# Agent attention and a gated feed-forward layer on one core: the SBUF tiles laid out in another order

## The chip, the cores and the metric

The kernel runs on 1 core of one Trainium2 chip. The metric is the device time of one execution in microseconds (us). The kernel before takes 1909.14 us, the median of 3 runs (1908.99 to 1910.31).

## What is computed

The reference, cut to what matters. Four batches of 12480 tokens, 128 channels, 49 agents; the 49920 result tokens go through a layer of width 2048.

```python
def sm(a, b):
    s = scale * (a @ b.transpose(0, 2, 1))
    s = s - s.max(-1, keepdims=True)
    e = np.exp(s)
    return e / (e.sum(-1, keepdims=True) + 1e-09)
agent_v = sm(agents, k) @ v
q2a = sm(q, agents)
x = (q2a @ agent_v).reshape(49920, 128)
h = x @ w_in
g = h * (1.0 / (1.0 + np.exp(-1.702 * h)))
return g @ w_out
```

## The kernel before

The kernel never forms the attention result x. For each batch it folds `agent_v` into the first weight matrix (`weights_part`, lines 492 to 507), so that a token's 49 softmax weights are multiplied with a 49 x 2048 matrix. Every float32 factor of the two large products is split in two parts (a rounded high part and the rest) and three products are added: high by high, low by high, high by low.

- **Up** (`up`, lines 580 to 593): for a chunk of 512 tokens and two slices of 128 of the 2048 columns, six matmuls into two PSUM banks `ph`. The weights `wh` and `wl` are the stationary operands, `hi`, `lo` (or their copies `hi2`, `lo2` with the halves of the partitions exchanged) the moving ones. Slice k stands on partitions k*64 to k*64+48, so the two matmuls of a pair work on the two halves of TensorE's rows.
- ScalarE applies the activation into `g` (line 591). `gh`, the rounded copy of `g`, comes from a DMA that POOL issues (line 601) or from ScalarE (line 603). VectorE makes `gl = g - gh` (line 609).
- **Down** (`down`, lines 612 to 619): twelve matmuls for two slices, weights `wo_h`, `wo_h`, `wo_l` against `gh`, `gl`, `gh`, again in pairs on the two halves of the rows, added up in `po`.
- Between these, in places that a table written out by hand sets, stand the softmax scores in bf16 pieces (line 241: `ag_part` against `qt`, `kt` and their remainders `rest`), the sum over the values (line 117 with `v_pair` and `e_pair`), a running maximum and the transposes of `p_pad`.

All these matmuls go through `on_rows` (line 117) or line 241. The engines' orders come from the order of the calls alone; no scheduler moves anything.

Every tile belongs to a pool. The pools lie in SBUF one behind another in the order in which they are opened, and inside a pool the tiles lie in the order in which they are first asked for, each rounded up to 32 bytes. So a tile whose size is no multiple of 256 bytes shifts everything that comes behind it modulo 256. Five such tiles stand in the pool `const`, more of them in the pool `work`:

```python
ag_sb = const.tile([P, B, A], F32, name="ag_sb")                    # 784 bytes a partition
v_pair = const.tile([P, KB, 2 * C + 2], F32R, name="v_pair")        # 8256
e_sb = const.tile([P, KB, A + 1], F32, name="e_sb")                 # 1600
score = const.tile([P, NKG * KB, A], F32, name="score")             # 20384
max_b = const.tile([P, A], F32, name="max_b")                       # 196
```

One tile walks through the bytes by itself: `v_pair` holds eight rows of 258 numbers, 1032 bytes each, and starts at byte 160 modulo 256. The eight matmuls of a group read them one after another, so their moving operands start at bytes 160, 168, 176, 184, 192, 200, 208 and 216 modulo 256. `score` does the same for VectorE: its slices for the 13 groups of keys begin 1568 bytes apart, so 32 further on modulo 256 each.

Of the kernel before, what the change touches and what calls it, by code (L numbers as in the profile page):

```python
# [8 lines left out]
F32 = mybir.dt.float32  # L9
F32R = mybir.dt.float32r  # L10
BF16 = mybir.dt.bfloat16
I32 = mybir.dt.int32
U32 = mybir.dt.uint32
# [5 lines left out]
P = 128  # L19
TB = 120  # L20
KB = 8
KG = TB * KB
QB = 128
CH = 512
# [25 lines left out]
def kernel(  # L50
# [11 lines left out]
    B, C, N = qT.shape  # L62
    A = agT.shape[2]
# [5 lines left out]
    NKG = N // KG  # L69
    H = P // 2  # L70
# [5 lines left out]
    def width(m):  # L76
        return min(CH, T - m * CH)
# [11 lines left out]
    const = ctx.enter_context(tc.tile_pool(name="const", bufs=1))  # L89
    wpool = ctx.enter_context(tc.tile_pool(name="wpool", bufs=2))  # L90
    loads = ctx.enter_context(tc.tile_pool(name="loads", bufs=3))
    work = ctx.enter_context(tc.tile_pool(name="work", bufs=2))
    gpool = ctx.enter_context(tc.tile_pool(name="gpool", bufs=3))
    ps_h = ctx.enter_context(tc.tile_pool(name="ps_h", bufs=4, space=bass.MemoryType.PSUM))
    ps_o = ctx.enter_context(tc.tile_pool(name="ps_o", bufs=1, space=bass.MemoryType.PSUM))
    ps_m = ctx.enter_context(tc.tile_pool(name="ps_m", bufs=1, space=bass.MemoryType.PSUM))
# [8 lines left out]
    def one_bank():  # L105
        return ps_h.tile([P, 512], F32, name="ph")

    def bank_pair(ps):
        ps = two_banks() if ps is None else ps
        return [ps[:, 0], ps[:, 1]]  # L110

    def rows(k, n=H):
        return slice(k * H, k * H + n)
# [2 lines left out]
        r = rows(k, n)  # L116
        nc.tensor.matmul(out=out, lhsT=lhsT[r], rhs=rhs[r], start=start, stop=stop, tile_position=(k * H, 0))  # L117

    ag_sb = const.tile([P, B, A], F32, name="ag_sb")
    nc.sync.dma_start(out=ag_sb, in_=agT)  # L120

    ident = const.tile([P, P], F32, name="ident")
# [5 lines left out]
    for i in range(2):  # L128
        t = const.tile([P, KB, P], F32R, name=f"e_pair{i}")
        nc.gpsimd.memset(t.bitcast(F32), 0.0)  # L130
        e_pair.append(t)
    v_pair = const.tile([P, KB, 2 * C + 2], F32R, name="v_pair")
    nc.gpsimd.memset(v_pair[:, :, 2 * C :].bitcast(F32), 1.0)
    p_pad = const.tile([P, KB // 2, P], F32, name="p_pad")
    nc.gpsimd.memset(p_pad, 0.0)


    e_sb = const.tile([P, KB, A + 1], F32, name="e_sb")
    nc.gpsimd.memset(e_sb[:, :, A:], EPS)

    w_in_sb = const.tile([P, F], F32, name="w_in_sb")
    wo_h = const.tile([P, NF, C], F32R, name="wo_h")
    wo_l = const.tile([P, NF, C], F32R, name="wo_l")
    score = const.tile([P, NKG * KB, A], F32, name="score")
    max_b = const.tile([P, A], F32, name="max_b")

# [5 lines left out]
    def to_float32(w, out):  # L154
        lo = w.rearrange("p n w -> p (n w)").bitcast(U16).rearrange("p (n w) -> p n w", w=4)[:, :, 1]
        hi = w[:, :, 1]
        ts = nc.vector.tensor_scalar
        stt = nc.vector.scalar_tensor_tensor

        ex = work.tile([P, 512], I32, name="ex", tag="rest")  # L160
        ts(out=ex.bitcast(U32), in0=hi, scalar1=20, scalar2=0x7FF, op0=ALU.logical_shift_right, op1=ALU.bitwise_and)
        yield
        ts(out=ex, in0=ex, scalar1=1023 - 127, scalar2=1023 + 128, op0=ALU.max, op1=ALU.min)
        yield
        ts(out=ex, in0=ex, scalar1=float(127 - 1023), scalar2=float(1 << 23), op0=ALU.add, op1=ALU.mult)
        yield
        stt(out=ex.bitcast(U32), in0=hi, scalar=0x80000000, in1=ex.bitcast(U32), op0=ALU.bitwise_and, op1=ALU.bitwise_or)
        yield

        m = work.tile([P, 512], U32, name="m21", tag="o", bufs=1)  # L170
        ts(out=m, in0=hi, scalar1=0xFFFFF, scalar2=0x100000, op0=ALU.bitwise_and, op1=ALU.bitwise_or)
        yield
        stt(out=m.bitcast(F32), in0=m, scalar=float(1 << 16), in1=lo, op0=ALU.mult, op1=ALU.add)
        yield
        stt(out=out, in0=m.bitcast(F32), scalar=2.0**-36, in1=ex.bitcast(F32), op0=ALU.mult, op1=ALU.mult)
# [3 lines left out]
    def convert(k, n=7):  # L179
        if k not in conversions:  # L180
            out, i = WORDS[k]
            conversions[k] = to_float32(words.pop(k), (wo_f if out else w_in_sb)[:, i * 512 : (i + 1) * 512])
        for _ in range(n):
            next(conversions[k], None)
# [10 lines left out]
        wo, s = quarter(i)  # L195
        nc.vector.tensor_sub(out=wo_l[:, s, :], in0=wo, in1=wo_h[:, s, :].bitcast(F32))

    ag_part = const.tile([P, B, 3, A], BF16, name="ag_part")

    def split_agents():  # L200
        rest = ag_sb
# [7 lines left out]
    def halves(t):  # L209
        w = t.bitcast(BF16).rearrange("p (n w) -> p n w", w=2)  # L210
        return w[:, :, 1], w[:, :, 0]
# [3 lines left out]
    def split(t):  # L215
        n = t.shape[1]
        half = n // 2
        if n == KG + PAD:
            half = (n + PAD) // 2
            nc.gpsimd.memset(t[:, KG:], 0.0)  # L220
        r = work.tile([P, n], F32, name="rest", tag="rest")

        def piece(i):
            s = slice(0, half) if i < 2 else slice(half, n)
            if i % 2 == 0:
                nc.vector.tensor_sub(out=r[:, s], in0=t[:, s], in1=halves(t)[0][:, s])  # L226
            else:
                nc.vector.tensor_sub(out=halves(r)[1][:, s], in0=r[:, s], in1=halves(r)[0][:, s])  # L228

        return (halves(t)[0], halves(r)[0], halves(r)[1]), piece  # L230
# [110 lines left out]
    def factors_0():  # L341
        m = work.tile([P, 1], F32, name="mcol", bufs=1)
        nc.vector.tensor_reduce(out=m, in_=first_m, axis=AX.X, op=ALU.min)
        ps = one_bank()
        nc.tensor.transpose(out=ps[:1, :P], in_=m, identity=ident)
        r = work.tile([P, 2, P], F32, name="mrow", tag="hi")
        nc.vector.tensor_copy(out=r[:1, 0], in_=ps[:1, :P])
        a, b = (r[:1, 0, k * H : (k + 1) * H].unsqueeze(1).broadcast_to([1, 2, H]) for k in range(2))
        nc.vector.tensor_tensor(out=r[:1, 1].rearrange("p (c a) -> p c a", c=2), in0=a, in1=b, op=ALU.min)
        return r  # L350
# [31 lines left out]
        return rz  # L382

    def divided(ps, rz):
        avT = work.tile([P, P], F32, name="avT", bufs=1)
        nc.vector.tensor_tensor(
            out=avT.rearrange("p (c a) -> p c a", c=2),
            in0=ps.rearrange("p (c a) -> p c a", c=2),
            in1=rz.unsqueeze(1).broadcast_to([P, 2, H]),
            op=ALU.mult,  # L390
        )
        return avT
# [157 lines left out]
    def query_pairs(g, ps=None):  # L550
        pp = p_pad
        ps = bank_pair(ps)
        hi, lo, hi2, lo2 = (work.tile([P, CH], F32R, name=x) for x in ("hi", "lo", "hi2", "lo2"))
        parts = []
        for k, n in enumerate((H, QB - H)):
            for i in range(KB // 2):
                nc.tensor.transpose(  # L557
                    out=ps[k][:, i * n : (i + 1) * n],
                    in_=pp[rows(k, n), i, :],
                    identity=ident[rows(k, n), rows(k, n)],  # L560
                    tile_position=(k * H, 0),
                )
            t = [x.rearrange("p (i t) -> p i t", t=QB)[:, :, rows(k, n)] for x in (hi, lo)]
            parts.append((ps[k][:, : KB // 2 * n].rearrange("p (i t) -> p i t", t=n), *t))
        for x, h, _ in parts:
            nc.scalar.copy(out=h, in_=x)
        return parts, hi, lo, hi2, lo2
# [58 lines left out]

    def store(m, po):
        n = width(m)
        o = work.tile([P, 2, CH], F32, name="o", tag="o", bufs=1)[:, :, :n]
        out = outT[:, m * CH : m * CH + n]  # L630
        if m == NC - 1:
            nc.scalar.copy(out=o[:, 0], in_=po[:, 0, :n])
            nc.vector.tensor_add(out=o[:, 0], in0=po[:, 1, :n], in1=o[:, 0])
            nc.sync.dma_start(out=out, in_=o[:, 0])
            return None
        nc.scalar.copy(out=o, in_=po[:, :, :n])  # L636
        nc.sync.dma_start(out=out, in_=o[:, 0])
        return o
# [31 lines left out]
    def do_key_split(b, g, i):  # L670
        if i == 0:
            k_parts[b, g], pieces[b, g] = split(kts.pop((b, g)))
        pieces[b, g](i)

    def do_query_split(n, i):
        if n < NG:
            if i == 0:
                q_parts[n], pieces[n] = split(qts.pop(n))
            pieces[n](i)
# [61 lines left out]
    with tc.manual_schedule(engines={E.PE, E.Activation, E.DVE, E.Pool, E.SP}):  # L741
# [1 line left out]
        first_m, first_z = first_mz[:, 0:KP], first_mz[:, KP:].rearrange("p (k i) -> p k i", i=3)  # L743
        nc.vector.memset(first_z, 0.0)
        nc.scalar.activation(out=first_m[:, 0:1], in_=first_z[:, 0, 0:1], func=AF.Exp)
        ag_0 = work.tile([P, H], F32, name="ag_0", tag="avT", bufs=1)
        nc.vector.memset(ag_0, 0.0)
        nc.vector.memset(sel, 0.0)
        nc.vector.tensor_copy(out=ag_0[:, 0:A], in_=ag_sb[:, 0, :])
# [20 lines left out]
        for p in range(KP):  # L770
# [13 lines left out]
            for i, (g, e) in enumerate(zip(first_groups(p), cols_e)):  # L784
                first_sums(p, g, e)
                if p == KP - 2 and i == 0:
                    r = factors_0()
                if p == KP - 2 and i == 1:
                    f = factors_1(r)
                    zc = first_zc(f)  # L790
                    acc = work.tile([P, 2, 2 * C + 1], F32, name="acc", bufs=1)[:, 0, 0:C]
                if p == KP - 1 and i == 0:
                    rz = first_rz(zc)
# [243 lines left out]
```

## Time and profile before

| | us |
|---|---|
| median of 3 runs | 1909.14 |
| the profiled execution | 1908.36 |
| its span, first to last instruction | 1906.6 |
| TensorE (PE) busy | 1883.1 |
| weight loads (PEld) busy | 1759.4 |
| VectorE (DVE) busy | 1537.3 |
| ScalarE (ACT) busy | 1492.3 |

The profile is of one execution, 0.04% below the median of the runs. A matmul's record lasts from its start to its modelled end, which lies about 160 ns behind the point where the next one of the same half can start; so two records overlap, and how fast matmuls follow one another is read from their starts, or from the time and the count of a stretch. The mean granted clock of TensorE was 0.999.

### The profile page before, as it was taken

How to read it: one execution, taken by the hardware profiler on the slowest of the kernel's cores; microseconds unless marked ns; L12 is line 12 of the kernel's file. 1: busy time of each engine (PE TensorE's matmuls, PEld its weight loads, DVE VectorE, ACT ScalarE, POOL GpSimd, SP SyncE). 2: the span in 40 equal slices, each digit the busy share in tenths (PEclk: the TensorE clock that was granted, in tenths of full speed). 3: DMA queues.
4: the chain of work that ended last, by engine and by line, in shares of the span. 5: the costliest groups of instructions: out<-in, count | busy, mean ns of one | idle time of the engine just before them, and what ended most of it. 6: DMA issues, size and time to landing. Idle time of an engine off the chain costs nothing.

```text
span 1906.6 us, 56411 instructions
## 1 busy us (share of the span) xinstructions
PE 1883.1 (99%) x24100; PEld 1759.4 (92%) x24100; DVE 1537.3 (81%) x1978; ACT 1492.3 (78%) x2410; POOL 335.5 (18%) x591
## 2 busy tenths in 40 slices
PE   7999999999999999999999999999999999999999
PEld 4678889999899999999999998999989999999999
DVE  7888998888688889888778888898867677767765
ACT  3677777888787777878777778777878788888886
POOL 1111111111111111111111111111111111111111
PEclk9999999999999999999999999999999999999999
DMA  9576767776567677777657777767655666666665
GB/s 362 171 223 211 210 203 205 212 215 199 169 207 208 209 206 209 214 205 204 203 173 207 210 211 200 214 203 207 191 170 178 192 196 184 197 186 193 195 179 145
DMA packets 133500, 384.96 MB, mean 202 GB/s; under 512 B 15125, under 2 KB 16789, under 8 KB 133249
## 3 DMA queue, kind: packets, MB, share of 16 engines
q0 software_dynamic: 77776, 254.98, 47.0%
q1 hardware_dynamic: 55473, 126.38, 19.8%
q8 instruction: 189, 3.10, 0.7%
q14 instruction: 62, 0.51, 0.1%
HBM read 81.53 MB, written 50.99 MB: 70 GB/s over the span
## 4 chain that ended last, share of the span: by engine, by line
PE 88%; DVE 6%; DMA 3%; issue 2%; ACT 2%; POOL 0%; SPq 0%; POOLq 0%; DVEq 0%; ACTq 0%
PE po L117 53%; PE ph L117 26%; PE ps_m L241 5%; DVE gl L609 2%; PE ps_m L117 2%; DMA kt<-kT 1%; DVE rest L226 1%; ACT g L591 1%; DVE rest L228 1%; DMA gh<-g 1%; PE ps_m L503 1%; PE ps_m L557 1%; DMA words<-w_out 0%; DVE score L254 0%; DMA lo<-lo 0%
## 5 line engine op out<-in xcount | busy, mean ns | idle before, releaser
L591 ACT ACTIVATE g<-ph 128x512 f32<-128x512 f32 x1568 | 807.7, 604 | 296.9 <-PE ph L117 285.8
L609 DVE TENSOR_TENSOR gl<-g,gh 128x1024 fp32r<-128x1024 f32 x776 | 924.4, 1215 | 79.9 <-ACT gh L603 56.2
L117 PE MATMUL po<-gh,wo_h 64*128 64x512 f32 (+1 forms) x3104 | 547.7, 398 | 0.0
L117 PE MATMUL po<-gl,wo_h 64*128 64x512 f32 (+1 forms) x3104 | 537.9, 393 | 1.9 <-DVE gl L609 1.9
L117 PE MATMUL po<-gh,wo_l 64*128 64x512 f32 (+1 forms) x3104 | 534.0, 390 | 0.0
L601 POOL DMA_DIRECT2D gh<-g x436 | 239.8, 551 | 1401.0 <-ACT g L591 1117.9
L117 PEld LDWEIGHTS po<-gl,wo_h 64*128 64x128 f32 x3104 | 367.6, 184 | 18.5 <-DVE gl L609 8.1
L117 PEld LDWEIGHTS po<-gh,wo_l 64*128 64x128 f32 x3104 | 369.9, 185 | 12.2
L117 PE MATMUL ph<-hi,wh 49*128 49x512 f32 (+4 forms) x1616 | 368.1, 387 | 0.3 <-DVE wl L507 0.3
L117 PE MATMUL ph<-lo,wh 49*128 49x512 f32 (+4 forms) x1616 | 367.6, 388 | 0.1
L117 PE MATMUL ph<-hi,wl 49*128 49x512 f32 (+4 forms) x1616 | 365.5, 384 | 0.0
L603 ACT CAST gh<-g 128x1024 fp32r<-128x1024 f32 (+1 forms) x340 | 357.6, 1053 | 9.0
L117 PEld LDWEIGHTS po<-gh,wo_h 64*128 64x128 f32 x3104 | 350.0, 185 | 13.8 <-issue 5.6
L117 PEld LDWEIGHTS ph<-hi,wh 49*128 49x128 f32 x1616 | 203.9, 184 | 11.1 <-ACT g L591 2.5
L117 PEld LDWEIGHTS ph<-lo,wh 49*128 49x128 f32 x1616 | 203.4, 184 | 7.2 <-DMA lo<-lo 0.6
L117 PEld LDWEIGHTS ph<-hi,wl 49*128 49x128 f32 x1616 | 203.3, 186 | 7.3 <-issue 0.7
L636 ACT COPY o<-po 128x1024 f32<-128x1024 f32 x97 | 98.3, 1013 | 62.2 <-PE po L117 62.2
L228 DVE TENSOR_TENSOR rest<-rest 128x512 bf16<-128x512 f32 (+2 forms) x176 | 129.9, 745 | 0.9
L241 PE MATMUL ps_m<-ag_part,rest 64*128 64x49 bf16 x4188 | 120.4, 181 | 0.3 <-DVE rest L228 0.3
L241 PEld LDWEIGHTS <-rest 64*128 64x128 bf16 (+1 forms) x4236 | 113.0, 94 | 0.6 <-DVE rest L228 0.4
L254 DVE TENSOR_TENSOR e_sb<-ps_m,e_sb 128x392 f32<-128x392 f32 x48 | 27.1, 565 | 97.2 <-ACT e_sb L253 97.2
L642 POOL DMA_DIRECT2D outT<-o x97 | 86.2, 888 | 91.4 <-DMA outT<-o 58.8
(143 smaller groups left out, 1324.9 us busy)
## 6 DMA issues: line engine op xcount, KB each, us to landing
gh<-g POOLq DMA_DIRECT2D x434, 512.0 KB, 3.5
kt<-kT SPq DMA_DIRECT2D x52, 480.0 KB
outT<-o SPq DMA_DIRECT2D x97, 256.0 KB
outT<-o POOLq DMA_DIRECT2D x97, 256.0 KB, 4.1
qt<-qT SPq DMA_DIRECT2D x94, 256.0 KB
vt<-v SPq DMA_DIRECT2D x39, 480.0 KB
hi<-hi SPq DMA_DIRECT2D x96, 98.0 KB
lo<-lo SPq DMA_DIRECT2D x96, 98.0 KB
```

Of the source, the lines that this page charges most:

```text
L117: nc.tensor.matmul(out=out, lhsT=lhsT[r], rhs=rhs[r], start=start, stop=stop, tile_position=(k * H, 0))
L226: nc.vector.tensor_sub(out=r[:, s], in0=t[:, s], in1=halves(t)[0][:, s])
L228: nc.vector.tensor_sub(out=halves(r)[1][:, s], in0=r[:, s], in1=halves(r)[0][:, s])
L241: nc.tensor.matmul(out=ps[k][o : o + n, j * A : (j + 1) * A], lhsT=x[r, t0 : t0 + n], rhs=ag_part[r, b, y, :], start=(i == 0), stop=(i == ...
L254: nc.vector.tensor_add(out=out, in0=h[1], in1=out)
L503: nc.tensor.matmul(out=pw[:, i * 256 : i * 256 + m], lhsT=w["avT"], rhs=w_in_sb[:, t : t + m], start=True, stop=True)
L591: nc.scalar.activation(out=g[:, k, :n], in_=ph[k][:, :n], func=AF.Gelu_apprx_sigmoid)
L601: nc.gpsimd.dma_start(out=gh, in_=g)
L603: nc.scalar.copy(out=gh, in_=g)
L609: nc.vector.tensor_sub(out=gl, in0=g, in1=gh.bitcast(F32))
L636: nc.scalar.copy(out=o, in_=po[:, :, :n])
L642: nc.gpsimd.dma_start(out=outT[:, m * CH : m * CH + width(m)], in_=o[:, 1], accum_op=ALU.add)
```

## The change

It alters where tiles lie in SBUF, and nothing else. Two pools are added: `lines` for those tiles of `work` whose sizes are multiples of 256 bytes, and `odd` for the tiles of `const` whose sizes are not. The order becomes `const`, `wpool`, `loads`, `lines`, `gpool`, `odd`, `work`. Tile sizes, buffer counts, dtypes, instructions, their order and what each waits for stay as they were.

```diff
     loads = ctx.enter_context(tc.tile_pool(name="loads", bufs=3))
+    lines = ctx.enter_context(tc.tile_pool(name="lines", bufs=2))
+    gpool = ctx.enter_context(tc.tile_pool(name="gpool", bufs=3))
+    odd = ctx.enter_context(tc.tile_pool(name="odd", bufs=1))
     work = ctx.enter_context(tc.tile_pool(name="work", bufs=2))
-    gpool = ctx.enter_context(tc.tile_pool(name="gpool", bufs=3))
...
-    ag_sb = const.tile([P, B, A], F32, name="ag_sb")
+    ag_sb = odd.tile([P, B, A], F32, name="ag_sb")
...
-    v_pair = const.tile([P, KB, 2 * C + 2], F32R, name="v_pair")
+    v_pair = odd.tile([P, KB, 2 * C + 2], F32R, name="v_pair")
...
-        r = work.tile([P, n], F32, name="rest", tag="rest")
+        r = lines.tile([P, n], F32, name="rest", tag="rest")
...
-        hi, lo, hi2, lo2 = (work.tile([P, CH], F32R, name=x) for x in ("hi", "lo", "hi2", "lo2"))
+        hi, lo, hi2, lo2 = (lines.tile([P, CH], F32R, name=x) for x in ("hi", "lo", "hi2", "lo2"))
...
-        o = work.tile([P, 2, CH], F32, name="o", tag="o", bufs=1)[:, :, :n]
+        o = lines.tile([P, 2, CH], F32, name="o", tag="o", bufs=1)[:, :, :n]
```

`e_sb`, `score`, `max_b` and `ag_part` go to `odd` too; `ex`, `m21`, `mrow` of the first batch, `avT` and `ag_0` go to `lines`. The first byte of the tiles, modulo 256, in the two built programs (all buffers of a tile share it, and the slices that matmuls read lie multiples of 256 bytes apart, but for `v_pair`, `qt`, `kt`, `rest` and `ag_part`):

| tile | read by | before | after |
|---|---|---|---|
| `wo_h`, `wo_l` | down, stationary | 32 | 128 |
| `gh`, `gl`, `g` | down, moving | 224 | 128 |
| `wh`, `wl` | up, stationary | 64 | 128 |
| `hi`, `lo`, `hi2`, `lo2` | up, moving | 160 | 128 |
| `wo_f` | first down steps, stationary | 64 | 128 |
| `e_pair` | values, stationary | 160 | 128 |
| `v_pair` | values, moving | 160 | 160 |
| `qt`, `kt` | scores, stationary | 64 | 128 |
| `rest` | scores, stationary | 224 | 128 |
| `ag_part` | scores, moving | 160 | 160 |
| `p_pad` | transposes | 224 | 128 |
| `w_in_sb` | folding the weights, moving | 32 | 128 |
| `o` | output | 96 | 128 |
| `e_sb` | softmax | 224 | 224 |
| `score` | softmax | 32 | 32 |

## Rows read from the trace of the kernel before

**Rows 1.** The page: span, then busy time, share of the span and instructions by engine.
```profile
span 1906.6 us, 56411 instructions
PE 1883.1 (99%) x24100; PEld 1759.4 (92%) x24100; DVE 1537.3 (81%) x1978; ACT 1492.3 (78%) x2410; POOL 335.5 (18%) x591
```

**Rows 2.** The page: the chain that ended last, share of the span by engine.
```profile
PE 88%; DVE 6%; DMA 3%; issue 2%; ACT 2%; POOL 0%; SPq 0%; POOLq 0%; DVEq 0%; ACTq 0%
```

**Rows 3.** Waits of PE: the two longest of them; us in total, times, longest.
```profile
PE ph L282 <- DMA kt<-kT: 10.6, 5, 8.7
PE po L117 <- DVE gl L609: 1.9, 6, 0.6
```

**Rows 4.** A stretch: width, busy us (instructions) of PE, PEld, DVE, ACT, POOL; granted clock; DMA.
```profile
300.00:1000.00 700.00, 699.92 (x8903) 661.19 (x8900) 586.66 (x746) 558.30 (x888) 124.89 (x216) 1.00 0.69 203
```

**Rows 5.** Groups by line and shape: count, busy us, mean ns of one, idle before.
```profile
L117 PE MATMUL po<-gh,wo_h 64*128 64x512 f32 x3072 | 543.9, 400 | 0.0
L117 PE MATMUL po<-gl,wo_h 64*128 64x512 f32 x3072 | 534.1, 394 | 1.7 <-DVE gl L609 1.7
L117 PE MATMUL po<-gh,wo_l 64*128 64x512 f32 x3072 | 530.3, 391 | 0.0
L117 PE MATMUL ph<-lo,wh 49*128 49x512 f32 x1504 | 347.9, 394 | 0.1
L117 PE MATMUL ph<-hi,wh 49*128 49x512 f32 x1504 | 347.7, 394 | 0.3 <-DVE wl L507 0.3
L117 PE MATMUL ph<-hi,wl 49*128 49x512 f32 x1504 | 345.0, 391 | 0.0
...
L117 PE MATMUL ph<-hi,wl 49*128 49x448 f32 x16 | 3.4, 363 | 0.0
...
L117 PE MATMUL ph<-hi,wl 49*128 49x256 f32 x16 | 2.9, 279 | 0.0
```

**Rows 6.** The chain in order of time, 718 to 728 us: start, us, what.
```profile
719.52 1.40 PE ph L117 x12
720.92 2.80 PE po L117 x24
```

**Rows 7.** PE's timeline and, for all of `wo_f`, durations in ns, min/median/max.
```profile
67.61 1.88 PE L117 MATMUL po<-g,wo_f 64*128 64x512 f32 x8
...
L117 PE MATMUL po<-g,wo_f x64: 587/589/693, 62.8 to 82.3; 64*128 64x512 f32 x64
```

**Rows 8.** The tile `v_pair` in one group: first matmuls, second to fourth, fourth to sixth, sixth to eighth.
```profile
L117 PE MATMUL ps_m<-v_pair,e_pair x2: 279/279/279, 348.5 to 348.5; 64*128 64x258 f32 x1, 56*128 56x258 f32 x1
...
L117 PE MATMUL ps_m<-v_pair,e_pair x6: 278/281/282, 348.6 to 348.9; 64*128 64x258 f32 x3, 56*128 56x258 f32 x3
...
L117 PE MATMUL ps_m<-v_pair,e_pair x6: 277/282/282, 348.9 to 349.1; 64*128 64x258 f32 x3, 56*128 56x258 f32 x3
...
L117 PE MATMUL ps_m<-v_pair,e_pair x6: 278/278/282, 349.1 to 349.4; 64*128 64x258 f32 x3, 56*128 56x258 f32 x3
```

**Rows 9.** Timeline of 597.6 to 598.1 us, and that pair of matmuls of `lo`, min/median/max.
```profile
597.63 0.25 PEld L117 LDWEIGHTS ph<-lo,wh 49*128 49x128 f32 x2
597.86 0.46 PE L117 MATMUL ph<-lo,wh 49*128 49x512 f32 x2
598.09 0.11 PEld L241 LDWEIGHTS <-qt 64*128 64x128 bf16 x2 [0.21 <-issue]
...
L117 PE MATMUL ph<-lo,wh x2: 393/393/393, 597.9 to 597.9; 49*128 49x512 f32 x2
```

**Rows 10.** The tile `gh` in matmuls from 716 to 728 us: durations, min/median/max.
```profile
L117 PE MATMUL po<-gh,wo_l x24: 388/391/395, 717.4 to 727.5; 64*128 64x512 f32 x24
```

**Rows 11.** Weight loads of the scores, and VectorE's softmax operations, by line and tile.
```profile
L241 PEld LDWEIGHTS <-rest 64*128 64x128 bf16 x4212 | 112.5, 93 | 0.6 <-DVE rest L228 0.4
...
L442 DVE TENSOR_TENSOR score<-score,max_b x39: 556/560/575, 256.6 to 1266.5; 120x392 f32<-120x392 f32 x39
...
L527 DVE TENSOR_TENSOR e_sb<-e_sb,m 128x392 f32<-128x392 f32 x49 | 27.8, 567 | 1.7
```

More of the change, by code (lines that the diff above doesn't have):

```diff
@@ L135 @@
     nc.gpsimd.memset(p_pad, 0.0)
-    e_sb = const.tile([P, KB, A + 1], F32, name="e_sb")
+    e_sb = odd.tile([P, KB, A + 1], F32, name="e_sb")
     nc.gpsimd.memset(e_sb[:, :, A:], EPS)
@@ L143 @@
     wo_l = const.tile([P, NF, C], F32R, name="wo_l")
-    score = const.tile([P, NKG * KB, A], F32, name="score")
-    max_b = const.tile([P, A], F32, name="max_b")
+    score = odd.tile([P, NKG * KB, A], F32, name="score")
+    max_b = odd.tile([P, A], F32, name="max_b")
     def load_words(src, i, queue):
@@ L158, in to_float32 @@
         stt = nc.vector.scalar_tensor_tensor
-        ex = work.tile([P, 512], I32, name="ex", tag="rest")
+        ex = lines.tile([P, 512], I32, name="ex", tag="rest")
         ts(out=ex.bitcast(U32), in0=hi, scalar1=20, scalar2=0x7FF, op0=ALU.logical_shift_right, op1=ALU.bitwise_and)
@@ L168, in to_float32 @@
         yield
-        m = work.tile([P, 512], U32, name="m21", tag="o", bufs=1)
+        m = lines.tile([P, 512], U32, name="m21", tag="o", bufs=1)
         ts(out=m, in0=hi, scalar1=0xFFFFF, scalar2=0x100000, op0=ALU.bitwise_and, op1=ALU.bitwise_or)
@@ L196, in down_weights_low @@
         nc.vector.tensor_sub(out=wo_l[:, s, :], in0=wo, in1=wo_h[:, s, :].bitcast(F32))
-    ag_part = const.tile([P, B, 3, A], BF16, name="ag_part")
+    ag_part = odd.tile([P, B, 3, A], BF16, name="ag_part")
     def split_agents():
@@ L345, in factors_0 @@
         nc.tensor.transpose(out=ps[:1, :P], in_=m, identity=ident)
-        r = work.tile([P, 2, P], F32, name="mrow", tag="hi")
+        r = lines.tile([P, 2, P], F32, name="mrow", tag="hi")
         nc.vector.tensor_copy(out=r[:1, 0], in_=ps[:1, :P])
@@ L384, in divided @@
     def divided(ps, rz):
-        avT = work.tile([P, P], F32, name="avT", bufs=1)
+        avT = lines.tile([P, P], F32, name="avT", bufs=1)
         nc.vector.tensor_tensor(
@@ L745 @@
         nc.scalar.activation(out=first_m[:, 0:1], in_=first_z[:, 0, 0:1], func=AF.Exp)
-        ag_0 = work.tile([P, H], F32, name="ag_0", tag="avT", bufs=1)
+        ag_0 = lines.tile([P, H], F32, name="ag_0", tag="avT", bufs=1)
         nc.vector.memset(ag_0, 0.0)
```

## The prediction

> **What bounds the kernel.** I read the page first. TensorE is busy for 1883.1 of 1906.6 us, VectorE for 81% and ScalarE for 78% [rows 1], and the chain of waits that ended last runs through TensorE for 88% of the span [rows 2]. TensorE's own waits are small: 10.6 us for the first keys at the start, 1.9 us in all for `gl` [rows 3]. In the long middle it has no gap at all, 699.92 busy us in 700, at a granted clock of 1.00, which is the 2.4 GHz level [rows 4]. So the time is the sum of TensorE's instructions, one behind another, and the order in which they stand is the same after the change. Anything that makes each one a few ns shorter or longer shows at full size; anything on the other engines hardly shows.
>
> Which instructions fill it: the 512-column matmuls of the two large products, 3 x 3072 + 3 x 1504 = 13728 of them [rows 5], in 6864 pairs (one of each pair on either half of the rows). How fast a pair follows the last: 24 matmuls of down in 2.80 us, 12 of up in 1.40 us [rows 6], so 2.80 / 12 = 1.40 / 6 = 0.2333 us a pair. 6864 x 0.2333 = 1601 us, 84% of the span. This one number carries the forecast: **1 ns a pair is 6.9 us**.
>
> Is there anything to win in it? At 2.4 GHz 512 columns are 213 ns. The plain float32 matmuls with `wo_f` show that such a stream can run without loss: eight of them, four pairs, take 1.88 us, of which the last record is 0.589 [rows 7], so (1.88 - 0.589) / 3 = 0.430 us a pair, twice 215. Their record is 589 - 430 = 159 ns longer than the pair's step, which is how I turn records into steps below. The pairs of the large products therefore lose 233.3 - 215 = 18 ns. Part of this grows with the columns: from 256 to 448 columns the record grows from 279 to 363 ns [rows 5], 0.4375 ns a column against 0.4167 at 2.4 GHz, which is 0.0208 x 512 = 10.7 ns. The other 7.6 ns do not grow with them.
>
> **The change, part by part.**
>
> *The large products.* All four kinds of operand move: `wo` from byte 32 modulo 256, `gh` and `gl` from 224, `wh` and `wl` from 64, `hi` and `lo` from 160, to byte 128. The nearest evidence is that the two products have been running at two different pairs of bytes all along: down with weights at 32 and stream at 224, up with weights at 64 and stream at 160. The distance from weight to stream is 192 in the one and 96 in the other, and both step at 233.3 ns [rows 6]. Weight loads are not what costs the 18 ns either: the last pair of `lo` before a block of scores has no load beside it (the last one ended at 597.88, the next begins at 598.09) and its records are 393 ns [rows 9], no shorter than the mean of 391 to 400 in rows 5. So neither the weight's byte nor its distance to the stream seems to matter. That leaves the stream's own first byte. Here the trace has only 160 and 224, both an odd multiple of 32, and `v_pair`, which walks in steps of 8. Its first matmul, at byte 160, has a record of 279; the second to fourth show 278, 281 and 282; the fourth to sixth 277, 282 and 282; the sixth to eighth 278, 278 and 282 [rows 8]. The 277 can only be the fifth, which starts at byte 192, the one even multiple of 32 among them. It is 2 ns under the first, 4 to 5 under its neighbours. But the fourth, just before it, is at 282, and a record ends where the next stream can begin: 282 + 277 is twice 279.5, the level of the whole group. It reads as a hand-over that falls a little later or earlier, not as time saved. I take **0 ns**, from rows 6, since they are of the very instructions that move. The bounds are -7.6 ns (the part that does not grow with the columns, all of it gone: -52 us) and +4 ns (every stream like the worst of `gh`, 395, instead of the median 391 [rows 10]: +27 us).
>
> By the Trainium skill ("SBUF — State Buffer", section Specifications) SBUF is read in lines of 16 bytes, and each cross to a new line costs something. Every operand above starts on a multiple of 32 before and after, so by that rule the sum changes by 0; by the 2 ns of rows 8 it would change by -14 us. That the odd multiples of 8 are the slower ones in rows 8 speaks for lines of some such size.
>
> *The other matmuls.* `v_pair` stays at byte 160; only its weights `e_pair` move, from 160 to 128. The scores load weights from `rest`, 93 ns each for 4212 of them [rows 11], beside matmuls whose moving operand `ag_part` stays. Zero for both; the bound is 1 ns for each of those loads, 4 us, if none of it were covered.
>
> *VectorE and ScalarE.* `score` steps through the bytes by 32 a slice, and its 39 subtractions take 556 to 575 ns, against 567 for the same shape in `e_sb` at a fixed byte 224 [rows 11]. No dependence, and at 81% and 78% busy a percent of their time is covered by TensorE. Were that cover gone, as for `gl` in rows 3, 1.9 us are at stake.
>
> *DMAs.* Number, size, queue and order are the same; only the SBUF side of each shifts. TensorE waited for them for 10.6 us at the start alone [rows 3], for transfers from HBM; a few percent of that is under 1 us either way.
>
> The sum: 1908.36 + 0 = 1908.4 us for the profiled execution, which stands 0.8 us under the median of the runs; so **1909 us**.
>
> **The rivals.**
>
> *Faster: the stream's start counts.* If a stream that starts and ends on an even multiple of 32 bytes really is shorter, each pair gains the 2 ns between 279 and 277 [rows 8]; that is 6864 x 2 = 14 us, 1895. With 4 ns, as against its neighbours or because 512 columns are twice 258, 27 us, 1881; with all 7.6 ns 52 us, 1856. For it: one byte of eight is the shortest, and no stream of the large products has had such a start yet. Against it: the neighbour that is longer by as much, and a sample of one byte, which is also not the byte 128 of the change. Chance 0.31, most of it between 1881 and 1905.
>
> *Much faster: the whole loss is one of place.* If the 18 ns came from starts at odd multiples of 32, a pair would step at 215: 6864 x 18.3 = 126 us, 1783. Against it: `v_pair` pays the same loss at all eight bytes (279 less 159 is 120 for 258 columns that need 107.5). Chance 0.04. The Trainium skill ("TensorE: Matmul & The Clock Gate", section Back-to-back issue gap) gives N / 2.4 + 2.5 ns for a warm stream, 216 for 512 columns. The float32 rows agree with it, the large products do not; by that rule alone the time would be some 119 us lower.
>
> *Slower: weight and stream collide.* Now every weight load reads from the same byte modulo 256 as the stream beside it. If SBUF served two readers at one place more slowly, each pair would go like the worst of rows 10, +4 ns: 27 us, 1936. The point from which it decides is half a ns a pair. Against it: distances 192 and 96 cost the same, a stream without a load beside it is no faster [rows 9], and the first matmul of `v_pair`, at distance 0 from `e_pair`, shows 279, in the middle of its group. For it: eight bytes of one small product are all there is of distances near 0. Chance 0.16, half of it under 1918.
>
> That the change does not do what it says can be excluded for the large products, by the table of bytes; it does not for `v_pair` and `ag_part`, which stay at 160, and which are a few percent of TensorE's time.
>
> **How the numbers follow.** A measurement tells 0.2%, 3.8 us, from no change; that is 0.55 ns a pair. No change within this: 0.49. Faster: 0.31 + 0.04 = 0.35. Slower: 0.16. The range goes from 1881 (the 4 ns of the first rival) to 1918 (half of the collision): it leaves out some 0.07 of the first rival, the 0.04 of the second and 0.08 of the third.
>
> **What would show it.** In the chain by time, 24 matmuls of down in 2.80 us and 12 of up in 1.40 us again, and groups at 391 to 400 ns. 2.77 and 1.385 instead would be the first rival, 2.58 the second, 2.85 the third. `v_pair` should show the same records, 277 to 282, in any case but a collision, where `e_pair` moves away from distance 0. If down and up part company, the forecast's reasoning that two pairs of bytes already stand for all was wrong.

## The result, and the profile after

The kernel after takes 1891.72 us, the median of 4 runs (1889.70 to 1891.86), against 1909.72 us for the kernel before on the same chip (1908.99 to 1911.57). The ratio is 0.9902 with an interval of 0.9885 to 0.9919: faster by 18 us. The forecast was no change. The profiled execution took 1891.72 us itself.

The page of the kernel after, against [rows 1] and [rows 2]: span, busy time by engine, and the chain that ended last.

```profile
span 1890.0 us, 56411 instructions
...
PE 1863.7 (99%) x24100; PEld 1742.1 (92%) x24100; DVE 1537.2 (81%) x1978; ACT 1492.6 (79%) x2410; POOL 333.8 (18%) x591
...
PE 88%; DVE 5%; DMA 3%; issue 2%; ACT 2%; POOL 0%; SPq 0%; POOLq 0%; DVEq 0%; ACTq 0%
```

The number of instructions is the same, VectorE and ScalarE are busy as long as before, and TensorE is busy for 19.4 us less. The chain still runs through TensorE for 88%. The waits of TensorE, against [rows 3]:

```profile
PE ph L284 <- DMA kt<-kT: 12.2, 6, 7.1
PE po L119 <- DVE gl L611: 2.7, 6, 0.7
```

They are 1.6 and 0.8 us longer than before. The waits for the keys lie in the first 54 us and took nothing back: the first matmul of the two large products starts at 54.24 us before and at 54.26 after. The gain came from the pace of the matmuls. The chain in order of time of the kernel after, 733 to 756 us (start, us, what), against [rows 6]:

```profile
733.01 1.39 PE ph L119 x12
...
740.31 2.74 PE po L119 x24
743.04 1.40 PE ph L119 x12
...
751.16 2.76 PE po L119 x24
755.31 2.75 PE po L119 x24
```

Down now needs 2.75 us for 24 matmuls where it needed 2.80: 229 ns a pair instead of 233. Up needs 1.39 instead of 1.40, 232 ns a pair. Over the whole trace, from the start of one 512-column matmul to the start of the next on the same half (steps of 245 ns and more, which contain a wait, left out), the mean step is 232.8 ns in down and 233.5 in up before, 229.0 and 231.5 after. Down has 4608 such pairs and up 2256, so the steps account for 4608 x 3.8 = 17.5 us and 2256 x 2.0 = 4.5 us. Some 3 us of these 22 went into longer steps with a wait, and some 2 us into the rest: by the starts of TensorE's matmuls from the first large one on, scores, values, transposes and the end together took that much more.

Where the step falls is seen in TensorE's timeline. One run of up and one of down in the kernel after (start us, duration, what):

```profile
717.97 0.52 PE L119 MATMUL ph<-hi,wh 49*128 49x512 f32 x2
...
719.36 0.75 PE L119 MATMUL po<-gh,wo_h 64*128 64x512 f32 x4
719.83 0.74 PE L119 MATMUL po<-gl,wo_h 64*128 64x512 f32 x4
720.29 0.74 PE L119 MATMUL po<-gh,wo_l 64*128 64x512 f32 x4
720.75 0.74 PE L119 MATMUL po<-gh,wo_h 64*128 64x512 f32 x4
721.20 0.74 PE L119 MATMUL po<-gl,wo_h 64*128 64x512 f32 x4
721.65 0.61 PE L119 MATMUL po<-gh,wo_l 64*128 64x512 f32 x3
```

Each line of four is two pairs. The starts lie 0.47, 0.46, 0.46, 0.45 and 0.45 us apart: the pace gets better along the run. In a run of down of the kernel before it does not; the starts lie 0.46 or 0.47 us apart to the end:

```profile
702.50 0.69 PE L117 MATMUL po<-gl,wo_h 64*128 64x512 f32 x4
702.97 0.69 PE L117 MATMUL po<-gh,wo_l 64*128 64x512 f32 x4
703.44 0.69 PE L117 MATMUL po<-gh,wo_h 64*128 64x512 f32 x4
703.90 0.69 PE L117 MATMUL po<-gl,wo_h 64*128 64x512 f32 x4
704.37 0.69 PE L117 MATMUL po<-gh,wo_l 64*128 64x512 f32 x4
704.83 0.47 PE L117 MATMUL ph<-hi,wh 49*128 49x512 f32 x2
```

Averaged over the trace of after by the place of a pair behind a switch from up to down (some 190 switches), the steps are 232.6, 235.6, 228.6, 232.3 and 230.8 ns, and from the sixth on flat at 227. Behind a switch from down to up the first five are the same within 0.2 ns, and up's run of six pairs is over when it reaches 227. So after the change a run **settles** at 227 ns within five steps, and every switch between the two sets it back. (Runs of down behind scores, values or transposes, most of which have a wait in them, come to 228 or less only from about the fourteenth pair on.) Before, nothing settles: from the fourth on, down's steps alternate between 235.4 and 231.2 ns to the end of each run.

The plain float32 matmuls with `wo_f` went from distance 160 (weights at 64, stream at 224) to 0 and did not move by a nanosecond, against [rows 7]:

```profile
L119 PE MATMUL po<-g,wo_f x64: 587/589/693, 62.8 to 82.3; 64*128 64x512 f32 x64
```

### The profile page after: what moved, and what is told of

Its sections match the earlier page's. It is cut to its first block, busy times and chain, and to the rows that moved or that the text cites. A ratio compares the mean times of both kernels' runs of the same rounds, so it can differ in the third digit from the quotient of the medians.

```text
span 1890.0 us, 56411 instructions
## 1 busy us (share of the span) xinstructions
PE 1863.7 (99%) x24100; PEld 1742.1 (92%) x24100; DVE 1537.2 (81%) x1978; ACT 1492.6 (79%) x2410; POOL 333.8 (18%) x591
## 4 chain that ended last, share of the span: by engine, by line
PE 88%; DVE 5%; DMA 3%; issue 2%; ACT 2%; POOL 0%; SPq 0%; POOLq 0%; DVEq 0%; ACTq 0%
PE po L119 52%; PE ph L119 26%; PE ps_m L243 5%; DVE gl L611 2%; PE ps_m L119 2%; DMA gh<-g 1%; DMA kt<-kT 1%; DVE rest L228 1%; ACT g L593 1%; PE ps_m L505 1%; DVE rest L230 1%; PE ps_m L559 1%; PE ph L284 0%; DMA lo<-lo 0%; DVE lo L573 0%
## 5 line engine op out<-in xcount | busy, mean ns | idle before, releaser
L119 PE MATMUL ph<-hi,wh 49*128 49x512 f32 (+4 forms) x1616 | 375.0, 389 | 0.3 <-DVE wl L509 0.3
L119 PE MATMUL ph<-hi,wl 49*128 49x512 f32 (+4 forms) x1616 | 372.9, 386 | 0.0
L119 PEld LDWEIGHTS ph<-hi,wh 49*128 49x128 f32 x1616 | 210.0, 184 | 11.8 <-ACT g L593 2.4
L119 PEld LDWEIGHTS ph<-lo,wh 49*128 49x128 f32 x1616 | 210.1, 185 | 6.8 <-DMA lo<-lo 0.8
L119 PEld LDWEIGHTS ph<-hi,wl 49*128 49x128 f32 x1616 | 209.6, 186 | 6.3 <-issue 0.7
```

## The experiments

Three theories could explain the sign. **A**, the first rival of the prediction: the stream's start on an even multiple of 32 counts. **B**: what counts is that weight and stream lie at one byte modulo 256, so their distance; the prediction had this effect with the other sign, as a collision. **C**: the byte of the weights counts. A kernel that only puts pools in another order tells them apart, since the table of bytes is known before it runs. All diffs are against the kernel after.

**Everything at byte 160** (`all160`): `ag_sb` goes back to the front.

```diff
-    ag_sb = odd.tile([P, B, A], F32, name="ag_sb")
+    ag_sb = const.tile([P, B, A], F32, name="ag_sb")
```

> The changed kernel with everything 32 bytes further on: all weights and streams at one byte again, 160, but an odd multiple of 32. Theory A (a stream that starts on an even multiple of 32 is shorter, whatever the weights do): the gain is gone, 1906 to 1912 us, records of the large products back at 391 to 400 ns. Theory B (one common byte for weight and stream is what counts, distance 0): unchanged, 1888 to 1894 us. Theory C (the weights' byte alone, even multiple of 32): 1906 to 1912 us.

1891.62 us (1890.98 to 1891.81), ratio 0.9909 [0.9893, 0.9924]. The chain by time:

```profile
759.97 2.75 PE po L119 x24
...
776.75 1.39 PE ph L119 x12
```

The pace of after, with every weight and stream at 160, where up's streams had been before. A and C fall; B stands.

**Weights alone at 160** (`w160`) and **streams alone at 160** (`m160`): distances from weight to stream of -32 and +32 modulo 256.

```diff
-    wo_h = const.tile([P, NF, C], F32R, name="wo_h")
-    wo_l = const.tile([P, NF, C], F32R, name="wo_l")
+    wo_h = wos.tile([P, NF, C], F32R, name="wo_h")
+    wo_l = wos.tile([P, NF, C], F32R, name="wo_l")
```

For the first, `ag_sb` lies ahead of `wos` and `wpool` and shifts both by 32, and `max_b` behind them shifts the rest back. For the second, `ag_sb` lies ahead of a pool `hl` for `hi`, `lo`, `hi2`, `lo2` and of `gpool`.

> The weights of both large products at 160, the streams still at 128. Theory A: unchanged, 1888 to 1894 us. Theory B: 1906 to 1912 us. Theory C: 1906 to 1912 us.

> The streams of both large products at 160, the weights still at 128. Theory A: 1906 to 1912 us. Theory B: 1906 to 1912 us. Theory C: unchanged, 1888 to 1894 us.

`w160`: 1908.88 us, ratio 0.9995 [0.9985, 1.0004]. `m160`: 1906.65 us, ratio 0.9989 [0.9980, 0.9999]. In the chain of `w160`:

```profile
756.10 1.40 PE ph L125 x12
758.47 2.80 PE po L125 x24
```

and in that of `m160`:

```profile
754.59 2.79 PE po L121 x24
757.38 1.40 PE ph L121 x12
```

32 bytes apart modulo 256 on either side, and the gain is gone, but for some 2 us in `m160`. Weights and streams at 128 and 128 or at 160 and 160 are fast, at 160 and 128 or at 128 and 160 slow. So it is not what lies at which byte, it is the distance between the two.

The period of 256 bytes is not shown by this. In the built programs of all fast kernels here the distance is a whole multiple of 512, and in `w160` and `m160` it is 224 and 288 modulo 512. No run has a distance of 256 modulo 512, so the period may as well be 512.

**Everything at byte 0** (`all0`), by small tiles ahead of `const`, which shift everything by 128 modulo 256.

```diff
-    max_b = odd.tile([P, A], F32, name="max_b")
+    max_b = sp224.tile([P, A], F32, name="max_b")
```

(`ag_part` goes ahead of `const` too, in a pool `sp160`; `m` and `z` in pools of their own behind `gpool`)

> Everything at byte 0 modulo 256, so weights and streams start at whole multiples of 256. Theories A, B and C: unchanged, 1888 to 1894 us. If lines larger than 128 bytes count, faster still: up to the 7.6 ns a pair that do not grow with the columns, 1857 us.

1888.88 us (1887.90 to 1891.08), ratio 0.9896 [0.9881, 0.9912], with steps of 229.1 and 231.5 ns. The interval overlaps that of after: byte 0, 128 or 160 makes no difference that these runs can tell.

**Distances 128 and 64** (`d128_64`): streams at 128, down's weights at 0, up's at 64.

```diff
-        m = work.tile([P, KB], F32, name="m")
+        m = mp.tile([P, KB], F32, name="m")
...
-    e_sb = odd.tile([P, KB, A + 1], F32, name="e_sb")
+    e_sb = ep.tile([P, KB, A + 1], F32, name="e_sb")
```

(small tiles ahead of the weights, `e_sb` behind them)

> Streams at 128 for both products; weights of down at 0 (distance 128), weights of up at 64 (distance 64). Theory B256 (only a distance of a whole multiple of 256 is fast): both products at 232.5 to 234 ns a pair, 1905 to 1911 us. Theory B128 (multiples of 128 will do): down at 229 ns, up at 233, 1892 to 1897 us. Theory B64 is nearly out already, since down had distance 192 before; it would give 1889 to 1894 us.

1903.27 us (1902.06 to 1904.50), ratio 0.9969 [0.9957, 0.9981]: a third of the gain. Down steps at 232.2 ns, up at 231.9, without a flat level at the end of a run. B in its plain form, all or nothing, does not say this, and the time lies between the two ranges that were given.

**One weight of three out of place** (`wl160`): only `wo_l` and `wl` at 160.

```diff
-            wts[b] = wpool.tile([P, F], F32R, name="wh"), wpool.tile([P, F], F32R, name="wl")
+            wts[b] = wpool.tile([P, F], F32R, name="wh"), wlp.tile([P, F], F32R, name="wl")
```

(and `wo_l` in a pool of its own)

> Only the low weights wo_l and wl at 160, the high ones and the streams at 128. This tells which weights meet the stream: those that the stream itself multiplies with, or those that are loaded beside it for the next one. Theory own: slow are the streams against wo_l and wl, a third of all, whatever comes next; those against wo_h before wo_l stay at 229 ns. Theory next: slow are the streams before a load of wo_l or wl (gl before wo_l, the first of gh against wo_l, hi against wh), the second gh against wo_l goes to 227 to 229 ns. By both a third of 18 us is given back: 1895 to 1900 us.

1901.38 us, ratio 0.9958 [0.9941, 0.9975]: a third of the matmuls out of place cost more than half of the gain. By transitions in down, the step from `gl` to the next `wo_l` matmul, during which `wo_l` is loaded, went from 229.3 in after to 234.0 ns; from one `wo_l` to the next from 228.5 to 231.8; from `wo_h` with `gh` to the next of the same, where nothing has been moved, from 229.7 to 232.5. The first of these rules out theory own. Theory next does not fit wholly either: the step from the second `wo_l` matmul to the next `wo_h`, which it put at 227 to 229 ns, is 231.0, and the time lies just over the range that both gave. The disturbance seems to be made in the pairs that have the weight out of place and carried on into those behind them, as the settling after a switch is.

**Fixed distance modulo 2048** (`gpar`): `gh` and `gl` have buffers of 4096 bytes; even and odd ones now go to two pools with 1024 bytes between them, so that down's distance modulo 2048 follows the loop.

```diff
-    ident = const.tile([P, P], F32, name="ident")
-    sel = const.tile([P, P], F32, name="sel")
+    ident = is_.tile([P, P], F32, name="ident")
+    sel = is_.tile([P, P], F32, name="sel")
...
-        gh = gpool.tile([P, 2, CH], F32R, name="gh", bufs=GH_BUFS)[:, :, :n]
+        gh = of_pair("gh", t).tile([P, 2, CH], F32R, name="gh", bufs=GH_BUFS // 2)[:, :, :n]
```

> The changed kernel with a spacer of 1024 bytes between the buffers of gh and gl for even and for odd steps, so that the distance from weight to stream modulo 2048 is 0 or 512 in all of down; in the changed kernel it is 1024 or 1536 in half of it. If the distance counts modulo 2048 (streams at 0 and 512 have stepped at 227 to 228.6 ns there, those at 1024 and 1536 at 229.5 to 232.5): 2300 pairs gain 3 ns, 1883 to 1887 us. If the step came from something else that goes with the steps' parity: 1888 to 1894 us.

1890.49 us, ratio 0.9902 [0.9887, 0.9916], step of down 229.0: nothing changes. Whether the distance is 0 or 512, or 1024 or 1536, modulo 2048 plays no part.

**Down alone at distance 0** (`downonly`): up's weights and streams back at a distance of 96.

```diff
-        hi, lo, hi2, lo2 = (lines.tile([P, CH], F32R, name=x) for x in ("hi", "lo", "hi2", "lo2"))
+        hi, lo, hi2, lo2 = (hl.tile([P, CH], F32R, name=x) for x in ("hi", "lo", "hi2", "lo2"))
```

(`hl` behind `ag_sb`, at 160; small tiles ahead of `wpool` put `wh` and `wl` at 64)

> The change made for down alone; up has its old bytes, weights at 64 and streams at 160. Theory B: down at 229 ns, up at 233.5 as before; 4600 pairs times 3.7 ns are saved, 1893 to 1898 us. If what counts is one byte for all operands of a stretch: slower, 1900 us or more.

1893.93 us (1893.52 to 1894.39), ratio 0.9920 [0.9905, 0.9935]. Down gives some 15 us of the gain, up the remaining 2 to 3: its runs of six pairs end where they would begin to pay.

**What sets a run back?** Up works on 49 rows of each half, down on 64. `rows64` runs up on 64 rows as well; rows 49 to 63 hold zeros. `rows64_before` is the same edit on the kernel before.

```diff
-                    on_rows(k, A, ph[k][:, lo:hi], ws[w][:, f], y[:, lo:hi], first, last)
+                    on_rows(k, H, ph[k][:, lo:hi], ws[w][:, f], y[:, lo:hi], first, last)
```

(and `hi2`, `lo2` are copied with H rows)

> The kernel after the change, with up's matmuls on 64 rows of each half instead of 49 (rows 49 to 63 hold zeros, so the sums are the same; the copies hi2 and lo2 move 64 rows too). Question: why do the pairs, with weight and stream at distance 0 modulo 256, take five steps of 232.6, 235.6, 228.6, 232.3 and 230.8 ns after every switch between up and down before they settle at 227 ns? Theory R (the number of rows, 49 against 64, changes at the switch): with 64 rows throughout the settling disappears, up's mean step falls from 231.4 to about 227 ns and down's from 229.0 to about 227 ns; 2288 pairs of up by 4.4 us per thousand is 6.6 us and 4576 of down by 2 ns 9 us: about 1875 us. Theory S (the switch itself, to other tiles and banks, sets it off): steps of 231.4 and 229.0 ns again, 1889 to 1894 us.

> The same edit on the kernel before the change. If the loss of the pairs is set by the distance of weight and stream modulo 256 alone (theory B), nothing changes: steps of 233 ns, 1906 to 1912 us. If the number of rows has a part in it by itself (more rows to load and stream), up's 2288 pairs change their step: 1 ns is 2.3 us; if the changes of row count cost some 25 ns each whatever the distance, 780 of them give 19 us back, 1890 us.

`rows64`: 1882.21 us (1880.62 to 1883.05), ratio 0.9863 [0.9848, 0.9877]. `rows64_before`: 1909.15 us, ratio 1.0004 [0.9994, 1.0014], with steps of 233 ns in both products. The chain of `rows64_before`:

```profile
327.69 2.80 PE po L117 x24
330.48 1.40 PE ph L117 x12
```

TensorE's timeline of `rows64`, a run of up and one of down:

```profile
755.98 0.43 PE L119 MATMUL ph<-hi,wh 64*128 64x512 f32 x2
...
757.34 0.66 PE L119 MATMUL po<-gh,wo_h 64*128 64x512 f32 x4
757.79 0.66 PE L119 MATMUL po<-gl,wo_h 64*128 64x512 f32 x4
758.25 0.66 PE L119 MATMUL po<-gh,wo_l 64*128 64x512 f32 x4
758.70 0.66 PE L119 MATMUL po<-gh,wo_h 64*128 64x512 f32 x4
759.15 0.66 PE L119 MATMUL po<-gl,wo_h 64*128 64x512 f32 x4
759.61 0.66 PE L119 MATMUL po<-gh,wo_l 64*128 64x512 f32 x4
760.06 0.43 PE L119 MATMUL ph<-hi,wh 64*128 64x512 f32 x2
```

Flat from the first line: six pairs of up in 1.36 us, twelve of down in 2.72, 227 ns a pair. Up's mean step fell from 231.5 to 227.0 ns, and the five slow steps behind a switch are gone. Theory R is right in its mechanism: at distance 0 the change of the row count sets a run back. It was wrong in its size, 9.5 us of the 16 it promised; its own figures even make 19, since 2288 pairs of up at 4.4 ns are 10 us and not 6.6. Up gave its 10 us. Down fell only from 229.0 to 228.1 ns, since its runs behind scores, values or transposes still begin at 231 to 233 ns, and the longer steps with a wait grew by some 3 us in all. One of the waits in `rows64`, 2.7 us in after:

```profile
PE po L119 <- DVE gl L611: 3.3, 6, 1.0
```

Without the equal bytes the same edit gives nothing. With them it beats both kernels: the interval of `rows64` lies wholly under that of after. It is 9.5 us lower by the medians, 7.4 by the ratios to the kernel before on the same chip.

**Sixteen bytes** (`d16`): `rows64` with down's weights 16 bytes on, in one tile that starts with four unused numbers.

```diff
+    wo_t = wos.tile([P, 2 * NF * C + 8], F32R, name="wo_t")
+    wo_h, wo_l = (wo_t[:, 4 + i * NF * C : 4 + (i + 1) * NF * C].rearrange("p (f c) -> p f c", c=C) for i in range(2))
```

(`ag_sb` and `max_b` share a tile, to make room)

> rows64 with the weights of down, wo_h and wo_l, shifted by 16 bytes (to byte 144 modulo 256, its streams gh and gl stay at 128); up stays at 128 and 128. Theory B in its narrow form (only the very same byte modulo 256 helps): down goes back to 233 ns a pair, 4576 x 5 = 23 us more than rows64, 1903 to 1907 us. Theory B in a wide form (weight and stream within one line of 32 or 64 bytes modulo 256): down stays at 228 ns a pair, 1879 to 1885 us. In between (a third to two thirds lost): the distance counts by degrees.

1890.00 us (1889.54 to 1891.06), ratio 0.9900 [0.9884, 0.9917]: in between, 7.8 us over `rows64`. But not by degrees. In the chain of `d16`:

```profile
321.10 2.79 PE po L119 x24
...
325.28 2.72 PE po L119 x24
...
334.86 2.72 PE po L119 x24
...
338.94 2.72 PE po L119 x24
```

Most runs are either at 2.72 us or at 2.79 and more. Of some 180 runs of down that follow up directly and have no wait in them, 163 step at 227 ns on average; of some 150 that come behind other work and have a step of 245 ns or more in them, about 110 step at 233 to 234 otherwise, where at distance 0 (`rows64`) 9 of as many do. So at 16 bytes the fast pace mostly holds once it is there, but most disturbed runs do not find back to it. Up, which stays at distance 0, steps at 228 ns here.

**Distances 128 and 64 on 64 rows** (`d128_64r`): both edits together.

> d128_64 (streams 128, weights of down at 0 and of up at 64) with up on 64 rows. Question: is the third of the gain that these distances gave a settled level of their own, or a part of the settling after the switches? If a level of their own: down and up at 231 to 232 ns a pair flat, 1901 to 1905 us as d128_64. If the switches of the row count broke up a better level there too: down falls towards 227 ns within each run of 24, 1882 to 1892 us. If they had lived from the switches: 233 ns, 1907 to 1911 us.

1902.13 us (1900.60 to 1903.65), ratio 0.9963 [0.9948, 0.9978]: as `d128_64`. Down steps at 232.3 ns (232.2 in `d128_64`) with no fall along a run, so at distance 128 the slower pace is not the switches' doing. Up, at distance 64, fell from 231.9 to 230.3 ns: there the switches had a small part.

## Why the prediction was right in its range and wrong in its forecast

- **The range and the forecast**: 1891.72 us lies in the range of 1881 to 1918, but the range was that wide to take in most of the first rival and half of the third. The forecast itself, no change and 1909 us, missed by 17 us, and the reasoning behind it failed. That the range held is luck as far as the mechanism goes: none of the rivals named the cause with the right sign.
- **What bounds the kernel**: right. The same 24100 matmuls, and their pace showed at nearly full size. By "1 ns a pair is 6.9 us" a mean step that is 3.2 ns shorter should give 22 us; 18 came.
- **The step that failed**: "So neither the weight's byte nor its distance to the stream seems to matter." With it the term of the large products was put at 0 ns a pair; it measured -3.8 in down and -2.0 in up. The sentence was drawn from two distances, 192 and 96, which step alike at 233.3 ns. The runs show 233 at -32 and +32 as well, 232 at 64 and 128, and at 0 229 in down (227 when settled) and 231.5 in up. The two that the kernel before had were both of the slow kind; two equal readings away from a special point say nothing of that point, and the change moved exactly there.
- **The second support of that step**, that a pair without a load beside it is no faster [rows 9], does not carry either. The last pairs of `lo` ahead of other work, 180 of them, some with and some without a load beside them, have records of 393 ns before and 385 after (median). In `wl160`, where that pair has its own weight at distance 0 but the pair before it has not, those without a load show mostly 393 and 394. So the pace seems to be carried over from the pairs before, and a missing load takes nothing away in that one pair.
- **`v_pair` at distance 0**, read against the collision, shows 279 in the middle of its group [rows 8]. It is one pair in eight, and a run of the large products needs five steps to settle. That may be too short for a gain or a loss to show; no run tests it. (Of the odd multiples of 8 in [rows 8], the eighth matmul, at byte 216, shows 278 and is not one of the slower ones.)
- **The first rival** had the sign and nearly the size (-2 ns a pair, 1895 us), but not the cause: `all160` has every stream at an odd multiple of 32 and is as fast. Of its marks, 2.77 and 1.385 us, the trace shows 2.75 and 1.39: down gains more and up less than one rule on the stream's start would give.
- **The third rival** named the right quantity, one place for weight and stream, with the wrong sign. By the Trainium skill ("TensorE: Matmul & The Clock Gate", section Step-by-step: what each phase is for) TensorE reads SBUF through two independent ports, one for the stream and one for the weights. By that the distance would make no difference at all; `w160` against `all160`, 1909 to 1892 us, differs, and the measurement decides.
- **The second rival**, 215 ns a pair: no kernel came near. The best settled level is 227, so 12 ns over the float32 rows stay unexplained.
- **"If down and up part company, the forecast's reasoning that two pairs of bytes already stand for all was wrong"**: they did, by 229 to 231.5 ns. The mark pointed to the right sentence, but by luck: both have the same distance now, and they part because up's runs of six pairs end just as they settle. With 64 rows in both, up is at 227.0 and down at 228.1.
- **The other parts**: VectorE, ScalarE, `wo_f` and the scores (116.2 us before and 116.3 after, from the start of each of their matmuls to the next start) did not change, as forecast. Of the waits of [rows 3], those for `gl` cost 0.8 us more.

What stays open: why a load from the stream's own byte goes beside it better. The runs show which distances do and how a run settles, not what happens inside. Open too is whether the period is 256 or 512 bytes, and which dtypes it holds for: all the pairs that changed are float32r with a weight load for each matmul, while the plain float32 ones with `wo_f` went to distance 0 and stayed as they were.

## What to carry to other kernels

Where long runs of matmuls bound a kernel, with a weight load for each, try weights and moving operands at one byte modulo 512, which is what the fast kernels had: it cost only the order of the pools and gave 1%. Keep the number of rows the same across the products that alternate, with zero rows if need be; with equal bytes that gave another 0.4 to 0.5%, without them nothing. And measure a pace by the place in a run, not only as a mean: the mean hid that a run only reached its pace at the sixth pair.

## What had not been expected of the hardware

- Matmuls have a memory. In one and the same kernel, after, a pair takes 227 to 236 ns depending on what ran up to five pairs earlier, at a granted clock of 1.00 from 100 to 1880 us.
- At a distance of 16 bytes there are two paces, 227 and 233 ns, and a run mostly keeps the one that it has; at 0 it goes to 227 from anywhere; at 32 either way modulo 256 it stays near 233.
- More work was faster: 64 rows instead of 49 in up, the added ones all zeros, took 9.5 us off the time.
